# Gates of the last two chunk pairs by seven block products instead of eight

## The chip, the core and the metric

The kernel runs on one core of a Trainium2 chip. The metric is the device time of one execution in microseconds (us), as a median of several runs. The engines of the core are TensorE (PE; PEld is its weight load), VectorE (DVE), ScalarE (ACT), GpSimd (POOL) and SyncE (SP), which here only issues DMAs. Each engine works through its own instructions in order, and an instruction waits for semaphores that others raise.

## What is computed

Linear attention with phi(x) = elu(x) + 1 over 8 batches, 8 heads, 576 positions and head size 64, and behind it a gated feed-forward block on the 4608 tokens of 512 features. Inputs and output are float32.

```python
q_p, k_p = (phi(q), phi(k))
kv = np.einsum('bhsd,bhse->bhde', k_p, v)
z = np.sum(k_p, axis=2)
num = np.einsum('bhsd,bhde->bhse', q_p, kv)
den = np.einsum('bhsd,bhd->bhs', q_p, z)[..., None] + 1e-06
x = (num / den)            # tokens x 512
a = x @ w1                 # 512 -> 1024
b = x @ w2                 # 512 -> 1024
h = a * b @ w3             # 1024 -> 1024
out = h @ w_out            # 1024 -> 512
```

## The kernel before

All matmuls take bfloat16 operands and sum into float32 in PSUM. The product w3 @ w_out is formed once at the start (steps T3 and FW), so each token then needs two gate matmuls (with w1 and w2), an elementwise product and one matmul with the folded 1024 x 512 weights.

The program is a list of steps written out by hand, `ORDER`. A step is a letter code with numbers: `F.5.0` is `s_F(5, 0)`. The last letter names an engine (a ACT, v DVE, p GpSimd; s and b name queues). The steps are issued in the list's order, and each engine keeps that order for its own instructions, so the list sets the order on every engine and in every queue.

- LQ, LK, LV load half a batch of q, k or v (576 KB) through SP's queue into one of 13 `ld` slots, which are handed round in order.
- PT, EX and PM form phi on DVE and ACT; VC casts v.
- KB (line 341, `kv_mm`) forms a batch's kv on TensorE. QD (line 386) transposes phi(q) by a DMA on SP's queue into a `qt` tile.
- NT and ND (line 399, `nd_mm`) form numerators and denominators of three tokens' tiles (128 tokens each) or one; NM (line 405, `over`) divides on DVE. Their PSUM tiles are the two `at` tiles of two banks each; four more `mm` tiles of one bank serve the rest.
- XD (line 463) transposes two tiles of x by a DMA on SP's queue: two XD make a chunk of 512 tokens, x transposed. There are nine chunks, 0 to 8.
- F.c.f (lines 483, 492, 494) makes 128 of the 1024 gate columns of chunk c: four matmuls for side a, four for side b, each 128 x 128 weights against 512 tokens; ACT copies a out of PSUM, and DVE multiplies it with b into `ab`. Chunk 0 is done in halves by FS.
- O.t (lines 536, 543) is one tile's eight matmuls with the folded weights and the copy out; S.t (line 549) stores it by two DMAs of 128 KB. Q.35 is the last tile, in pieces.

In the list F steps of a chunk stand where its two XD are expected to be through, and the loads, phi, KB and NT of later batches are spread between them up to chunk 6.

Of the kernel before, what the change touches and what calls it, by code (L numbers as in the profile page):

```python
# [19 lines left out]
T3.7.0.v LO.0 CO.0.a LO.2 CO.1.v FW.2.0.a T3.7.1.a LO.3 FW.4.0.a CO.3.a LQ.0.0 L3.6 FW.7.0.a  # L23
PT.q.0.0 L3.1 FW.2.1.a FW.4.1.a EX.q.0.0 LQ.0.1 PM.q.0.0 CO.2.p FW.2.2.a FW.7.1.a FW.7.2.v FW.7.3.a
FW.4.2.a FW.4.3.v QP.0.0.v C3.6.a LK.0.0 T3.1.0.a T3.1.1.a PT.q.0.1 FW.2.3.v L3.3 L3.5 T3.6.0.v
T3.6.1.v EX.q.0.1 LK.0.1 FW.1.0.a FW.1.1.a PT.k.0.0 FW.1.2.a PM.q.0.1 FW.6.0.a FW.6.1.v FW.6.2.v
LH.0.0 EX.k.0.0 T3.3.0.a T3.3.1.a FW.1.3.a C3.5.v T3.5.0.a FW.6.3.v EX.k.0.1 PT.k.0.1 LV.0.0 LV.0.1
LH.0.1 FW.3.0.a FW.3.1.v T3.5.1.a FW.3.2.v FW.3.3.v PM.k.0.1 LA.0 LB.6 I.2 CA.0.p CB.6.p LB.7
PM.k.0.0 T3.0.0.a LA.1 FW.5.0.a VC.0.0.a QP.0.1.v FW.0.0.a FW.0.1.a KV.0.0.a LA.2 VC.0.1.v FW.5.1.v
T3.0.1.v KV.0.1.a NT.0 NM.0.0 NM.0.1 CB.7.p FW.0.2.a FW.0.3.a NM.0.2 FW.5.2.a FW.5.3.a LA.3 XP.0.a  # L30
CA.2.p XP.1.v ND.3 LB.2 CA.1.v XP.2.a LB.3 FS.0.0.0.0 FS.0.1.0.0 FS.0.1.1.0 FS.0.0.1.0 LQ.1.1 LK.1.0
XP.3.v FS.0.2.0.0 FS.0.2.1.0 FS.0.2.0.1 FS.0.2.1.1 CB.2.v FS.0.0.0.1 FS.0.0.1.1 FS.0.1.0.1
FS.0.1.1.1 FS.0.3.0.1 CB.3.v PT.q.1.1 CA.3.p F.0.4 EX.q.1.1 PM.q.1.1 PT.k.1.0 LQ.1.0 LV.1.0 PT.q.1.0
EX.k.1.0 FS.0.3.0.0 LK.1.1 F.0.5 F.0.6 PM.k.1.0 VC.1.0.v EX.q.1.0 PM.q.1.0 QP.1.1.a EX.k.1.1
FS.0.3.1.0 PT.k.1.1 LV.1.1 F.0.7 KV.1.0.a LQ.2.1 LQ.3.1 VC.1.1.a QP.1.0.a O.0.a PM.k.1.1 KV.1.1.v
LV.2.0 FS.0.3.1.1 EX.q.3.1 NT.4 NM.4.0 NM.4.1 O.1.a NM.4.2 EX.q.2.1 PT.q.2.1 LK.2.0 XP.4.a ND.7
XP.5.a LK.2.1 EX.k.2.1 LK.3.1 O.2.a PT.q.3.1 PT.k.2.1 LV.3.0 XP.6.v XP.7.v LV.2.1 EX.k.2.0 PM.k.2.1
LV.3.1 O.3.a PT.k.2.0 LQ.2.0 S.0.s LQ.3.0 PM.k.2.0 PM.q.2.1 VC.2.0.v LV.4.1 F.1.0 F.1.1 PT.k.3.1
# [26 lines left out]
def kernel(  # L65
# [36 lines left out]
    def take(kind, key, shape, dtype, name):  # L102
        if kind in free:
            s = slots[key] = free[kind].popleft()
        else:
            s = taken.get(kind, 0) % turns[kind]
            taken[kind] = taken.get(kind, 0) + 1
        pool = ps if kind in ("mm", "at") else sb
        return pool.tile(shape, dtype, tag=f"{kind}{s}", name=name)

    def give(kind, key):
# [415 lines left out]
    def s_FP(c0, f, side, g, e):  # L527
        f_mm(c0, f, side, slice(2 * g, 2 * g + 2))
        if g == 1:
            f_out(c0, f, side)  # L530

    def o_mm(t, cols):
        c0, m = divmod(t, CT)
        o_ps = mm_tile("o_ps")[:, 0:cols.stop - cols.start]
        for f in range(FC):
            nc.tensor.matmul(o_ps, abs_[c0][:, f, m * P:(m + 1) * P], wf_sb[:, f, cols],  # L536
                             start=(f == 0), stop=(f == FC - 1))
# [66 lines left out]
```

## Time and profile before

| | |
|---|---|
| time, median of 3 runs | 240.42 us (240.42 to 240.85) |
| span of the profiled execution | 239.7 us |
| around the span, up to the median | 0.7 us |
| bytes moved by DMA | 55.81 MB |
| read from HBM, written | 38.80 MB, 9.44 MB |

The profile is of one execution. Its views name an engine, a line of the kernel, what is written and what is read (`ab<-a_sb,b_ps`), shapes as partitions x elements, a count, the busy time and the mean time of one in ns, and the idle time before it with what ended that. A chain row has its start, its length, the work and a count. A row of busy times by stretch has for PE, PEld, DVE, ACT, POOL the busy us and the count, then the granted TensorE clock (1.00 is full), the busy share of the 16 DMA engines (which can pass 1 where transfers overlap) and GB/s. A row of waits has who waited for whom: us in total, times, longest. Issue rows of DMAs give KB each and the median us from issue to landing.

### The profile page before, as it was taken

The numbers are of one execution on the slowest core, as the hardware profiler recorded it, in microseconds if no ns is written. First come the engines' busy times: TensorE is split into PE (matmuls) and PEld (weight loads), VectorE is DVE, ScalarE is ACT, GpSimd is POOL, SyncE is SP. The second block draws the span as 40 slices with busy tenths as digits, with TensorE's granted clock in tenths as the row PEclk, the third lists the DMA queues.
The fourth block names the chain that finished last, engine by engine and source line by source line (L and its number), as shares of the span: only waits on it lengthen the run. The fifth ranks groups of instructions, "written<-read, shape, count | busy, mean of one in ns | idle before, by whom it ended". The sixth has DMA issues, their size and how long they took to land.

```text
span 239.7 us, 5540 instructions
## 1 busy us (share of the span) xinstructions
PE 233.2 (97%) x2276; PEld 120.2 (50%) x2276; DVE 151.0 (63%) x278; ACT 115.0 (48%) x173; POOL 8.1 (3%) x15
## 2 busy tenths in 40 slices
PE   8899999999999999999999999999999999999994
PEld 5656668555445444444454444545444444444443
DVE  0347787889999646877862588885546363433341
ACT  2576743979793255568522656424232113321300
POOL 1020053000000000000000000000000000000000
PEclk9999999999999999999999999999999999999999
DMA  6999999999996999999879959965293763005216
GB/s 241 402 406 397 379 375 390 390 390 389 396 332 137 158 357 247 323 406 296 190 106 192 392 123 262 320 116 131 52 178 69 174 157 88 3 0 125 50 24 154
DMA packets 52553, 55.81 MB, mean 233 GB/s; under 512 B 31280, under 2 KB 32560, under 8 KB 52528
## 3 DMA queue, kind: packets, MB, share of 16 engines
q1 hardware_dynamic: 52288, 55.19, 78.5%
q8 instruction: 18, 0.29, 0.5%
q10 hardware_dynamic: 240, 0.26, 0.3%
q14 instruction: 7, 0.06, 0.1%
HBM read 38.80 MB, written 9.44 MB: 201 GB/s over the span
## 4 chain that ended last, share of the span: by engine, by line
PE 96%; DVE 1%; ACT 1%; issue 0%
PE o_ps L536 26%; PE a_ps L483 25%; PE b_ps L483 24%; PE wf_ps L264 6%; PE nd L399 3%; PE w3p L252 3%; PE warm L149 2%; PE kbp L341 2%; PE a_ps L516 2%; PE b_ps L516 2%; PE xp L458 1%; PE qp L369 1%; PE kvp L341 1%; ACT wo_sb L218 0%; ACT w3b L238 0%; DVE w3t L253 0%
## 5 line engine op out<-in xcount | busy, mean ns | idle before, releaser
L483 PEld LDWEIGHTS <-w_sb 128*128 128x128 bf16 x544 | 52.6, 98 | 62.5 <-DVE xt L459 0.3
L494 DVE TENSOR_TENSOR ab<-a_sb,b_ps 128x512 bf16<-128x512 f32 x68 | 46.2, 686 | 39.9 <-PE b_ps L483 38.6
L492 ACT COPY a_sb<-a_ps 128x512 f32<-128x512 f32 x68 | 39.8, 586 | 64.0 <-PE a_ps L483 63.6
L483 PE MATMUL a_ps<-xt,w_sb 128*128 128x512 bf16 x272 | 69.9, 380 | 0.0
L483 PE MATMUL b_ps<-xt,w_sb 128*128 128x512 bf16 x272 | 69.8, 379 | 0.0
L536 PE MATMUL o_ps<-wf_sb,ab 128*128 128x512 bf16 (+2 forms) x304 | 65.2, 368 | 0.0
L536 PEld LDWEIGHTS <-ab 128*128 128x128 bf16 x304 | 28.4, 98 | 31.7 <-issue 0.4
L543 ACT COPY o_sb<-o_ps 128x512 f32<-128x512 f32 x22 | 12.9, 586 | 33.5 <-PE o_ps L536 26.7
L405 DVE TENSOR_TENSOR xn<-nd,r 128x512 bf16<-128x512 f32 (+2 forms) x47 | 23.8, 559 | 0.3
L274 ACT ACTIVATE ek<-k 128x1152 bf16<-128x1152 f32 x16 | 18.7, 1172 | 0.7 <-ACT ek L274 0.7
L274 ACT ACTIVATE eq<-q 128x1152 bf16<-128x1152 f32 x16 | 18.7, 1168 | 0.4 <-DMA q<-in_q_dram 0.4
L543 DVE COPY o_sb<-o_ps 128x512 f32<-128x512 f32 x13 | 9.0, 691 | 15.3 <-PE o_ps L536 12.6
L264 PE MATMUL wf_ps<-wo_sb,w3t 128*128 128x512 bf16 x64 | 15.6, 380 | 0.5 <-ACT wo_sb L218 0.5
L286 DVE TENSOR_SCALAR phq<-q 128x1152 bf16<-128x1152 f32 x16 | 12.0, 755 | 2.7 <-DMA q<-in_q_dram 2.7
L294 DVE TENSOR_TENSOR phk<-phk,ek 128x1152 bf16<-128x1152 bf16 x16 | 11.9, 750 | 1.8 <-ACT ek L274 1.7
L294 DVE TENSOR_TENSOR phq<-phq,eq 128x1152 bf16<-128x1152 bf16 x16 | 12.1, 755 | 1.0 <-ACT eq L274 0.8
L286 DVE TENSOR_SCALAR phk<-k 128x1152 bf16<-128x1152 f32 x16 | 12.0, 753 | 0.0
L264 PEld LDWEIGHTS <-w3t 128*128 128x128 bf16 x64 | 5.9, 98 | 5.8 <-issue 0.7
L328 ACT CAST vt<-v 128x1152 bf16<-128x1152 f32 x7 | 8.1, 1162 | 0.9 <-DMA v<-in_v_dram 0.9
L253 ACT CAST w3t<-w3p 128x512 bf16<-128x512 f32 x7 | 4.0, 587 | 9.3 <-PE w3p L252 7.4
L399 PEld LDWEIGHTS <-qt 64*64 64x64 bf16 x576 | 6.1, 106 | 4.3 <-issue 4.1
L399 PE MATMUL nd<-kv,qt 64*64 64x65 bf16 x576 | 7.6, 194 | 0.4 <-DVE w3t L253 0.4
(57 smaller groups left out, 127.4 us busy)
## 6 DMA issues: line engine op xcount, KB each, us to landing
q<-in_q_dram SPq DMA_DIRECT2D x16, 576.0 KB, 8.3
k<-in_k_dram SPq DMA_DIRECT2D x16, 576.0 KB, 9.5
v<-in_v_dram SPq DMA_DIRECT2D x16, 576.0 KB, 10.5
out_dram<-o_sb SPq DMA_DIRECT2D x69, 128.0 KB, 2.5
w<-in_moe_w_dram SPq DMA_DIRECT2D x7, 512.0 KB, 10.9
wo<-in_moe_w_out_dram SPq DMA_DIRECT2D x4, 512.0 KB, 8.2
wa<-in_moe_w_dram SPq DMA_DIRECT2D x4, 512.0 KB, 10.7
wb<-in_moe_w_dram SPq DMA_DIRECT2D x4, 512.0 KB, 10.4
```

Source lines behind the costliest of these rows:

```text
L264: nc.tensor.matmul(wfs[i], w3ts[i][:, c, :], wo_sb[:, c, :], start=(c == 0), stop=(c == FC - 1))
L274: nc.scalar.activation(out=t, in_=raw[n, b, h], func=AF.Exp)
L286: (nc.gpsimd if e == "p" else nc.vector).tensor_scalar(out=by_set(n, t), in0=by_set("k", raw[n, b, h]), scalar1=0.0, scalar2=1.0, op0=ALU. ...
L294: nc.vector.tensor_tensor(out=t, in0=t, in1=by_set("k", es[n, b, h]), op=ALU.min)
L399: nc.tensor.matmul(dst[g * R:(g + 1) * R], qts[b, a // 2][rows, j, a % 2 * R:(a % 2 + 1) * R], kvs[b][rows, a // 2, a % 2, :], start=True, ...
L405: nc.vector.tensor_tensor(out=xn[:, :, a0:a1], in0=n4[:, :, :, 0:D], in1=r.unsqueeze(3).to_broadcast([P, 2, a1 - a0, D]), op=ALU.mult)
L483: nc.tensor.matmul(ops_[key][:, tiles.start * P:tiles.stop * P], w[:, w_row(kc), f * P:(f + 1) * P], xts[c0][:, tiles, kc, :], start=(kc = ...
L492: nc.scalar.copy(out=a_sbs[c0, f], in_=ops_[key])
L494: nc.vector.tensor_mul(out=abs_[c0][:, f, :], in0=a_sbs[c0, f], in1=ops_[key])
L516: nc.tensor.matmul(p, w[:, w_row(kc), f * P:(f + 1) * P], xts[c0][:, 2 * g:2 * g + 2, kc, :], start=(kc == 0), stop=(kc == KC - 1))
L536: nc.tensor.matmul(o_ps, abs_[c0][:, f, m * P:(m + 1) * P], wf_sb[:, f, cols], start=(f == 0), stop=(f == FC - 1))
L543: copy_of(e)(out=o_sbs[t], in_=o_ps)
```

## The change

Chunks 5 and 6, and 7 and 8, form two pairs. For a pair the gate of 256 columns (f and f + 4) by 1024 tokens over the 512 features is a product of 2 x 2 blocks on each side. The change forms it in Winograd's way of Strassen's method: seven products of blocks and sums of blocks in place of eight. A product (`WP.c.f.side.i`) is two matmuls of 128 x 128 weights against 512 tokens.

- WS forms four sums of weight blocks for each side, in bfloat16, on DVE (for w1 into the tile of w_out, which is no longer needed; for w2 into `ld` slots). WT forms four differences of blocks of x per pair.
- One PSUM bank takes products 1, 6, 7 and 4 of a side on top of one another (y), one takes 5 and 3 (z), one of the `mm` banks takes 2 (x). After 1, 5 and 6 ACT copies the bank out; after 2, 3 and 7 DVE adds such a copy to the bank; after 4 ACT copies (side a) or DVE multiplies (side b). A product into a bank waits for the read of what is there.
- The products of the other three blocks, a times b, have both factors in SBUF: they are on GpSimd (24 of them). The results go into `ld` slots (`abq`), from which O reads.
- RB closes the pool of the two `at` tiles and opens four one-bank tiles (`bk`) in their place, for y and z.

The list of steps is the same up to the load of q that follows step PT.k.2.0, and another one behind it.

```diff
+PAIRS = (5, 7)
+WIDE = ()
...
-    free = {"ld": deque(range(13)), "mm": deque(range(4)), "at": deque(range(2))}
+    at_pool = ctx.enter_context(ExitStack())
+    pools = {"mm": ps, "at": at_pool.enter_context(tc.tile_pool(name="at", bufs=1, space=bass.MemoryType.PSUM))}
...
+    free = {"ld": deque(range(13)), "mm": deque(range(4)), "at": deque(range(2)), "bk": deque(range(4))}
...
-            nc.tensor.matmul(o_ps, abs_[c0][:, f, m * P:(m + 1) * P], wf_sb[:, f, cols],
+            nc.tensor.matmul(o_ps, ab_of(c0, f)[:, m * P:(m + 1) * P], wf_sb[:, f, cols],
...
+    def s_WS(side, i, e):
+        w = (w1_sb, w2_sb)[side]
+        a, b, op = {1: (w_half(w, 0, 1), w_half(w, 1, 1), ALU.add),
+                    2: (ws_of(side, 1), w_half(w, 0, 0), ALU.subtract),
+                    3: (w_half(w, 0, 0), w_half(w, 0, 1), ALU.subtract),
+                    4: (w_half(w, 1, 0), ws_of(side, 2), ALU.subtract)}[i]
+        (nc.gpsimd if e == "p" else nc.vector).tensor_tensor(out=ws_of(side, i), in0=a, in1=b, op=op)
+
+    def s_WT(c0, i, e):
+        b11, b12, b21, b22 = x_half(c0, 0), x_half(c0 + 1, 0), x_half(c0, 1), x_half(c0 + 1, 1)
+        a, b = {1: (b12, b11), 2: (b22, xs_of(c0, 1)), 3: (b22, b12), 4: (b21, xs_of(c0, 2))}[i]
+        (nc.gpsimd if e == "p" else nc.vector).tensor_tensor(out=xs_of(c0, i), in0=a, in1=b, op=ALU.subtract)
+
+    def w_mm(ps, c0, f, side, i, first):
...
+        for r in range(2):
+            nc.tensor.matmul(ps, lhs[:, r, f * P:(f + 1) * P], rhs[:, :, r, :],
+                             start=(first and r == 0), stop=(r == 1), skip_group_check=not first)
...
+    def w_add(c0, f, side, ps, tmp, c, g, e):
+
+        nc.vector.tensor_tensor(out=tmp, in0=ps, in1=tmp, op=ALU.add)
+        if side == 0:
+            wtmp[c0, f, "a", c, g] = tmp
+        else:
+            (nc.gpsimd if e == "p" else nc.vector).tensor_mul(
+                out=w_ab(c0, f, c, g), in0=wtmp.pop((c0, f, "a", c, g)), in1=tmp)
+
+    def s_RB(e):
+
+        at_pool.close()
+        pools["bk"] = at_pool.enter_context(tc.tile_pool(name="bk", bufs=1, space=bass.MemoryType.PSUM))
+
+    def s_WP(c0, f, side, i, e):
+        q = c0, f, side
+        bank = q + ("z" if i in (3, 5) else "x" if i == 2 else "y",)
...
+        w_mm(ps, c0, f, side, i, i in (1, 2, 5))
+        if i in (1, 5, 6):
+            t = wtmp[q + (i,)] = w_tmp({1: "e", 5: "phq", 6: "phk"}[i], "p" + str(i) + "ab"[side])
+            nc.scalar.copy(out=t, in_=ps)
+        elif i == 2:
+            w_add(c0, f, side, ps, wtmp.pop(q + (1,)), 0, 0, e)
+            give("mm", bank)
+        elif i == 3:
+            w_add(c0, f, side, ps, wtmp.pop(q + (6,)), 1, 0, e)
+            give("bk", bank)
+        elif i == 7:
+            w_add(c0, f, side, ps, wtmp.pop(q + (5,)), 1, 1, e)
+        elif side == 0:
+            t = wtmp[c0, f, "a", 0, 1] = w_tmp("a_sb", "p4a")
+            nc.scalar.copy(out=t, in_=ps)
+        else:
+            nc.vector.tensor_mul(out=w_ab(c0, f, 0, 1), in0=wtmp.pop((c0, f, "a", 0, 1)), in1=ps)
```

In the list itself the part around the start of the new stage reads:

```diff
+XD.6.0 NM.30.1 NM.30.2 O.18.a WS.1.4.v NT.33 NM.33.0 WT.5.1.v WT.5.3.v WT.5.2.v NM.33.1 NM.33.2 RB
+WP.5.0.0.1 O.19.a WP.5.0.0.5 WP.5.0.1.5 XD.7.1 WP.5.0.0.2 WP.5.0.1.1 WP.5.0.0.6 WT.5.4.v WP.5.0.0.3
```

and the gates of chunks 1 to 4 stand on TensorE in the order F.1.5 F.1.7 F.1.1 F.1.2 F.1.4 F.1.6 ND.8 KB.2 F.1.0 F.1.3 NT.9 KB.3 O.7 O.6 NT.12 O.5 O.4 F.2.7 NT.15 F.2.5 F.2.6 F.2.2 F.2.4 F.2.3 F.2.1 F.3.4 F.2.0 F.3.7 KB.4 O.8 F.3.5 F.3.0 NT.18 KB.5 F.3.3 O.10 F.3.6 F.3.1 NT.21 O.9 O.11 F.4.6, then F.4.0 F.4.4 F.4.5 KB.6 NT.24 F.4.1 F.3.2 F.4.2 F.4.3 O.13 NT.27 KB.7 F.4.7 NT.30 O.15 O.18 NT.33 and the first product.

On SP's queue, between the third store of the program and the second pair of x transposes, there stood before (q, k, v are loads, o_sb stores, qt the transposes of phi(q), QD, and xt those of x, XD):

```order
L549 DMA out_dram<-o_sb 64x512 x4
L386 DMA_TRANSPOSE qt<-phq 128x9x128 x4
L463 DMA_TRANSPOSE xt<-xn 128x8x128 x2
L158 DMA v<-in_v_dram 128x2x576
L158 DMA q<-in_q_dram 128x2x576
L549 DMA out_dram<-o_sb 64x512 x2
L158 DMA k<-in_k_dram 128x2x576
L158 DMA q<-in_q_dram 128x2x576
L158 DMA k<-in_k_dram 128x2x576
L463 DMA_TRANSPOSE xt<-xn 128x8x128 x2
```

The two pairs of xt here are XD.2 and XD.3, with five loads between them. In the change the same stretch of SP's queue, from the first QD of batch 2 to the first half of XD.3, reads:

```order
L401 DMA_TRANSPOSE qt<-phq 128x9x128 x2
L173 DMA q<-in_q_dram 128x2x576 x2
L401 DMA_TRANSPOSE qt<-phq 128x9x128 x2
L173 DMA q<-in_q_dram 128x2x576
L478 DMA_TRANSPOSE xt<-xn 128x8x128
L576 DMA out_dram<-o_sb 64x512 x2
L478 DMA_TRANSPOSE xt<-xn 128x8x128
L173 DMA v<-in_v_dram 128x2x576
L173 DMA k<-in_k_dram 128x2x576 x4
L173 DMA v<-in_v_dram 128x2x576
L478 DMA_TRANSPOSE xt<-xn 128x8x128
```

Loads of later batches have moved ahead of the transposes: three between the QD and XD.2, six between XD.2 and XD.3, and the transposes stand singly. From the load of q at which the lists part up to XD.4.1, 25 loads stand in the queue in the change; up to XD.4.1 of before 17 do.

On TensorE, at the end of NT.33 (nd is its PSUM tile, qt a weight), there stood before the output matmuls of O.26:

```order
L399 LDWEIGHTS qt
L399 MATMUL nd<-kv,qt 64x65
L536 LDWEIGHTS ab
L536 MATMUL o_ps<-wf_sb,ab 128x512
L536 LDWEIGHTS ab
```

In the change NT.33 is followed by the first product, into bank y of side a (wya), and then by O.19; the semaphores that an instruction waits for stand in brackets:

```order
L414 MATMUL nd<-kv,qt 64x65
L642 LDWEIGHTS w_sb [waits DMAHW7_49,DMAHW2_49,DVE_49]
L642 MATMUL wya<-xt,w_sb 128x512 [waits PE_49]
L642 LDWEIGHTS w_sb
L642 MATMUL wya<-xt,w_sb 128x512
L557 LDWEIGHTS ab
L557 MATMUL o_ps<-wf_sb,ab 128x512 [waits Activation_49]
```

The weight load in front of the first product now waits for DVE; its count is that of the last division of NT.33. What DVE has there is, from NT.33's first instruction on:

```order
L446 TENSOR_SCALAR r<-nd 128x14
L447 TENSOR_SCALAR r<-nd 128x10
L448 RECIPROCAL r<-r 128x24
L420 TENSOR_TENSOR xn<-nd,r 128x512
L631 TENSOR_TENSOR xs<-xt 128x1024 x2
L631 TENSOR_TENSOR xs<-xt,xs 128x1024
L420 TENSOR_TENSOR xn<-nd,r 128x2x192
L420 TENSOR_TENSOR xn<-nd,r 128x2x64
L420 TENSOR_TENSOR xn<-nd,r 128x512
L662 TENSOR_TENSOR p1a<-wxa,p1a 128x512
```

Three WT differences (xs) have come between the divisions (xn) of NT.33; before, the same divisions stood together.

More of the change, by code (lines that the diff above doesn't have):

```diff
@@ L27 @@
[L27 to L38, printed above, removed]
@@ L107, in take @@
             taken[kind] = taken.get(kind, 0) + 1
-        pool = ps if kind in ("mm", "at") else sb
+        pool = pools.get(kind, sb)
         return pool.tile(shape, dtype, tag=f"{kind}{s}", name=name)
@@ L530, in s_FP, with ab_of @@
             f_out(c0, f, side)
+    def ab_of(c0, f):
+        for c in range(2):
+            if c0 - c in PAIRS and c0 - c not in WIDE:
+                return quads[c0 - c, f % 4][:, c, f // 4]
+        return abs_[c0][:, f]
     def o_mm(t, cols):
@@ L544, in s_O @@
         give("mm", "o_ps")
+        c0 = t // CT - (t // CT - 1 in PAIRS)
+        if c0 in PAIRS and c0 not in WIDE:
+            n = uses["o", c0] = uses.get(("o", c0), 0) + 1
+            if n == 2 * CT:
+                for f in range(FC // 2):
+                    give("ld", ("abq", c0, f))
     def store(queues, t, o_sb, cols):
@@ new lines, in w_tmp, with w_ab @@
+    def w_tmp(kind, name):
+        if kind == "a_sb":
+            return take(kind, None, [P, NCH], F32, name)
+        t = take(kind, None, [P, HW], BF16, name)
+        return t.bitcast(F32)[:, 0:NCH]
+    def w_ab(c0, f, c, g):
+        if c0 in WIDE:
+            if c0 + c not in abs_:
+                abs_[c0 + c] = take("ab", None, [P, FC, NCH], BF16, "ab")
+            return abs_[c0 + c][:, f + 4 * g]
+        if (c0, f) not in quads:
+            quads[c0, f] = late(("abq", c0, f), 4).rearrange("p (c g n) -> p c g n", c=2, g=2)
+        return quads[c0, f][:, c, g]
```

115 lines of the change are left out of this document (89 added, 26 removed).

## The prediction

> **What bounds the kernel now.** I read the page first (busy shares, the chain that ended last), then the busy time by stretch, then what TensorE waited for, then the chain in order of time.
>
> ```profile
> span 239.7 us, 5540 instructions
> PE 233.2 (97%) x2276; PEld 120.2 (50%) x2276; DVE 151.0 (63%) x278; ACT 115.0 (48%) x173; POOL 8.1 (3%) x15
> PE 96%; DVE 1%; ACT 1%; issue 0%
> ```
> ```profile
> 60.00:80.00 20.00, 20.00 (x291) 9.88 (x290) 18.94 (x34) 13.45 (x22) 0.00 (x0) 1.00 0.98 270
> 120.00:140.00 20.00, 20.00 (x219) 9.45 (x205) 10.91 (x24) 8.08 (x14) 0.00 (x0) 1.00 0.88 209
> 200.00:220.00 20.00, 20.00 (x95) 9.00 (x93) 7.52 (x11) 5.26 (x9) 0.00 (x0) 1.00 0.12 28
> ```
> ```profile
> PE warm L149 <- DVE zero L136: 1.2, 1, 1.2
> PE wf_ps L264 <- ACT wo_sb L218: 0.5, 1, 0.5
> ```
>
> The reader is to see that TensorE is full: 20.00 of 20 us in each stretch (first column after the length), at granted clock 1.00, and that its longest wait in all, 1.2 us, is the first one. The time is the sum of TensorE's own work, so fewer matmuls shorten it as long as nothing makes TensorE wait. The columns behind are DVE, ACT and GpSimd busy time, then clock, DMA share and GB/s: from 60 to 80 us DVE (18.94 of 20) and the DMA engines (0.98) are nearly full too. That is where the change moves work to.
>
> **What the seven products save.**
>
> ```profile
> 203.30 0.86 PE a_ps L483 x4
> 103.22 1.73 PE o_ps L536 x8
> 119.57 0.78 PE kbp L341 x72
> 190.59 0.51 PE nd L399 x48
> 59.93 0.86 PE a_ps L483 x4
> ```
>
> These rows of the chain (start, length, count) price each TensorE step: four gate matmuls 0.86 us, so 0.216 each; a gate step F (both sides) 1.73; an output step O 1.73; KB 0.78; NT 0.5. A pair of chunks takes 2 x 64 gate matmuls before and 4 blocks x 2 sides x 7 products x 2 = 112 in the change. Two pairs save 32 x 0.216 = **6.9 us**. O, KB, NT and the rest keep their counts.
>
> **What it adds beside TensorE.**
>
> ```profile
> L494 DVE TENSOR_TENSOR ab<-a_sb,b_ps 128x512 bf16<-128x512 f32 x68 | 46.2, 686 | 39.9 <-PE b_ps L483 38.6 <-ACT a_sb L492 0.8 <-issue 0.3
> L294 DVE TENSOR_TENSOR phk<-phk,ek 128x1152 bf16<-128x1152 bf16 x16 | 11.9, 750 | 1.8 <-ACT ek L274 1.7
> L492 ACT COPY a_sb<-a_ps 128x512 f32<-128x512 f32 x68 | 39.8, 586 | 64.0 <-PE a_ps L483 63.6
> L222 POOL CAST w_sb<-wa 128x1024 bf16<-128x1024 f32 x3 | 3.3, 1085 | 18.9 <-DMA wa<-in_moe_w_dram 18.9
> ```
>
> Per block of 28 matmuls (6.05 us of TensorE) ACT makes 7 copies at 586 ns, 4.1 us, and DVE six sums and one product out of PSUM at 686, 4.8 us. Both fit under 6.05. The 24 products of two SBUF tiles on GpSimd are not in the trace: the nearest row is its cast of 1024 columns at 1.09 us, so 0.54 for 512 columns from below and, with two fp32 inputs, 1.09 from above. I take 1.09, the whole row: three a block, 3.3 us, also hidden; they would show only beyond 2.0 each. The 16 block sums (WS, WT, 1024 bf16 columns) are priced by the 1152-column bf16 row: 750 x 1024/1152 = 0.67 us, from above twice the 512-column row, 1.37. I take 0.67, the same kind of operation.
>
> In the Strassen stage a product is two matmuls, 0.43 us, and one bank is written, read, and written again (1, 6, 7, 4). A read-back costs about 0.9 us from matmul to reader's end (0.69 and the handover), and the order keeps two or more other products between a pair that depends so; where DVE is one operation late TensorE loses up to 0.69. Nothing from below, 16 such chains x 0.69 = 11 from above; DVE has 56 x 0.686 + 4 x 0.67 + 8 copies x 0.69 = 46.6 us of work beside 48.4 us of products and 13 O steps, 70.9 in all, so I take **0.8**, near the empty end.
>
> **What it moves: the transfers.** All of NT and KB now stands ahead of the stage, so the loads of K, Q and V, and the DMA transposes behind them, have to be done some 25 us of TensorE work earlier. They share one queue, in which transposes stand behind loads.
>
> ```profile
> 40.00:70.00 30.00, 30.00 (x385) 16.03 (x384) 27.00 (x51) 25.62 (x37) 0.00 (x0) 1.00 1.05 391
> 75.00:77.00 2.00, 2.00 (x80) 1.10 (x81) 2.00 (x4) 0.52 (x1) 0.00 (x0) 1.00 0.00 0
> 92.00:94.00 2.00, 2.00 (x11) 0.89 (x10) 1.03 (x2) 0.82 (x2) 0.00 (x0) 1.00 1.44 89
> ```
> ```profile
> 52.20 1.19 SPq L158 DMA_DIRECT2D q<-in_q_dram  x1
> ```
> ```profile
> v<-in_v_dram SPq DMA_DIRECT2D x2, 576.0 KB, 12.1
> ```
> ```profile
> DMA packets 2593, 0.65 MB, mean 259 GB/s; under 512 B 2593, under 2 KB 2593, under 8 KB 2593
> ```
>
> To be seen: the DMA engines are full to 70 us, at 391 GB/s; a load of 576 KB costs 1.51 us, a tile's two stores (256 KB) 0.67. The last row is the stretch from 72.0 to 74.5 us, in which only transposes ran, at 259 GB/s: 1.14 us for a phi tile (QD, 295 KB), 1.01 for a half x chunk (XD, 262 KB). The load issued at 52.20 is the last before the orders part; its neighbours landed 12.1 us after issue, so it lands at 64.3. From 75 to 77 the queue of before is empty: room that the change fills.
>
> Going from transposes back to loads costs more: from 92 to 94 only 89 GB/s moved. So 0 to 1.5 us a switch; I take 0.6, nearer to nothing, because the change issues most transposes one by one with loads already queued behind them.
>
> Up to XD.2.1, which F.2.7 needs, the change queues 9 loads, 3 store pairs, 4 QD, 2 XD, 2 switches: 13.6 + 2.0 + 4.6 + 2.0 + 1.2 = 23.4, so it lands at 87.7. TensorE would be there at 59.93 (quoted row, F.1) + 8 F + 4 O + ND + 2 KB + 2 NT = 83.5: **4.2 late**. Up to XD.3.0, which F.3.4 needs: 7 loads, 1 pair, 2 XD, 2 switches more, 14.5, so 102.2 against 83.5 + 7 F + NT = 96.1: 6.1 late. Up to XD.4.1, which F.4.6 needs: 9 loads, 5 pairs, 4 QD, 2 XD, 5 switches, 26.6, so 128.8 against 96.1 + 8 F + 4 O + 2 KB + 2 NT = 119.4: **9.4 late** in total (the delays contain each other). Without any price for switches it is 123.4, 4.0 late; at 1.5 each 136.9, 17.5 late. Behind it the queue has under 20 us of work for 24 us of TensorE, so nothing more is late.
>
> **The wait that it adds.** RB closes the pool of the two-bank tiles; the first product's weight load then waits for DVE's last read of them, NM.33.2, and all of TensorE's queue stands behind it, O.19 first, which needs nothing of it.
>
> ```profile
> 191.24 0.16 DVE L431 TENSOR_SCALAR r<-nd 128x14 f32<-128x14 f32 x1
> 191.32 0.16 DVE L432 TENSOR_SCALAR r<-nd 128x10 f32<-128x10 f32 x1
> 191.51 0.30 DVE L433 RECIPROCAL r<-r 128x24 f32<-128x24 f32 x1
> 191.85 1.95 DVE L405 TENSOR_TENSOR xn<-nd,r 128x512 bf16<-128x512 f32 x4
> ```
>
> Before, NT.33 ends at 191.1 on TensorE and DVE is through with it at 193.8, 2.7 us later; O.26 hides that. In the change three WT sums (2.0) stand between its parts and nothing hides it: **4.7 us**. From below 2.7 + 3 x 0.6 = 4.5; with sums at 1.37 it is 6.8.
>
> **Sum.** The profiled execution's span is 239.7; 0.7 lies around it up to the median of 240.4, and I let that stay. 240.4 - 6.9 + 9.4 + 4.7 + 0.8 = **248.4 us**.
>
> **Rivals.**
> - *The transfers keep up.* If transposes don't wait for the loads ahead, or the queue packs better than 391 GB/s, so that XD.4.1 lands by 119.4, only the wait at RB is left: 240.4 - 6.9 + 4.7 + 0.8 = 239.0, faster. For it: in the trace no x chunk comes late. Against: the order of before has that empty queue at 75, and 17 loads ahead of XD.4 where the change has 25; it decides where 25 loads, 9 pairs, 8 QD and 6 XD take under 55.1 us (64.3 to 119.4), and without a switch they cost 59.0. Chance 0.15.
> - *Everything is covered,* RB too, since DVE reads NM.33 before TensorE is there: 240.4 - 6.9 = 233.5 to 236. Against: NM.33 needs NT.33, the instruction just ahead. Chance 0.04.
> - *Switches at full price, and a stage held by DVE.* 17.5 late, 6.8 at RB, 3 in the stage: 240.4 - 6.9 + 27.3 = 260.8; with one of them, 254 to 257. For it: from F.1 to NM.33 DVE has 32 gate products x 0.69, 52 operations of 1152 columns x 0.75, 9 NT x 2.6 and 11 block sums x 0.67, 92 us less some overlap of neighbours, in 84 us of TensorE, so a late load is hard to make up. Chance 0.13.
> - *The gates are not fewer in time* (a product's two matmuls at other than 0.43): their shapes are those of L483, so I give it no chance of its own.
>
> One rule speaks against GpSimd's part. In the trace GpSimd is idle (0.00) in all stretches after 40 us, so no row shows it beside DVE. The Trainium skill, SBUF — State Buffer, section "Who interferes with whom", says that a Vector instruction with two SBUF inputs and a GpSimd instruction that reads SBUF exclude each other for the whole instruction. Here that would touch the four WT sums inside the stage alone (the other DVE sums have one input in PSUM): at most 4 x 1.09 = 4.4 us of DVE, in a stage where it has 24 to spare, and if all of it reached TensorE 252.8. It lies inside the range, at a chance of 0.03.
>
> **How the numbers follow.** Forecast 0.65 (242.5 to 254), with 0.15, 0.04, 0.13 and 0.03 as above. The range of 8 in 10 leaves out the fast end below 239 and the far end above 256: **239 to 256**. A measurement tells about 0.2% from no change. Faster 0.17 (the two fast rivals, less a little of the first), same 0.03, slower 0.80.
>
> **What would show it.** Saving: 512 gate matmuls of 128x512 in place of 544, still 216 ns apart. Transfers: TensorE's waits name DMA xt, ahead of F.2.7, F.3.4 and F.4.6, some 9 us together, and the DMA share stays near 1 from 72 to 125 us. RB: one wait of about 4.7 us on DVE xn ahead of the first product. Stage: ACT and DVE under 75% busy, few waits on p tiles. I am wrong if TensorE has no wait on xt (then 239), or if the waits within the stage pass 5 us together.

## The result and the profile after

| | before | after |
|---|---|---|
| time, median (four runs each, on one chip) | 240.57 us (240.42 to 240.85) | 258.38 us (257.44 to 260.57) |
| ratio | | 1.0739, 95% interval 1.068 to 1.0799 |
| span of the profiled execution | 239.7 us | 256.7 us (its own time 258.76) |

The change makes the kernel 7.4% slower. The sign was forecast, the size was not: 258.4 against 248.4, and outside the range of 239 to 256. Ratios leave out runs in a slower state that some executions show, which matters for the sixth experiment alone: two of its four runs, the profiled one among them, were in it.

First the page of the changed kernel: span, TensorE's busy share, the granted clock in 40 slices (tenths), and who stands on the chain that ended last.

```profile
span 256.7 us, 5592 instructions
PE 230.5 (90%) x2244; PEld 117.5 (46%) x2244; DVE 177.0 (69%) x318; ACT 127.4 (50%) x197; POOL 38.9 (15%) x39
PEclk9999999999999999997999999799999999999998
PE 70%; DMA 14%; DVE 10%; issue 2%; ACT 1%; SPq 1%; DVEq 0%; ACTq 0%
```

TensorE is busy for 2.7 us less than before, but over a span 17.0 longer. It is no longer alone on the chain, where transfers now hold 14% and DVE 10%, and in two slices its clock falls.

Then what TensorE waited for from F.1 to RB (first fence) and behind that (second): who for whom, us in total, times, longest.

```profile
PE nd L414 <- DMA qt<-phq: 4.1, 3, 2.0
PE a_ps L498 <- DMA xt<-xn: 3.6, 2, 1.9
PE kbp L356 <- DVE ab L509: 2.1, 2, 1.8
PE b_ps L498 <- DVE ab L509: 1.9, 2, 1.6
```
```profile
PE wya L642 <- DVE xn L420: 4.6, 1, 4.6
PE wya L642 <- DVE xs L631: 0.9, 1, 0.9
PE wya L642 <- DVE p5a L662: 0.6, 1, 0.6
```

Last, five stretches of the changed kernel (from the first matmul of F.1 to that of F.4.6, on to the end of NT.33, the wait at RB, the stage up to the last matmul, and the end), and the end of the kernel before.

```profile
59.13:133.70 74.57, 62.84 (x794) 29.65 (x793) 62.07 (x115) 43.13 (x61) 0.00 (x0) 0.98 1.12 303
133.70:158.77 25.07, 24.76 (x432) 12.33 (x432) 19.54 (x42) 10.53 (x17) 0.00 (x0) 1.00 0.76 144
158.77:163.35 4.58, 0.00 (x2) 0.00 (x1) 4.29 (x10) 0.11 (x1) 0.00 (x0) 0.94 0.89 191
163.35:251.75 88.40, 86.94 (x408) 39.46 (x408) 51.12 (x76) 34.96 (x63) 30.91 (x24) 0.98 0.28 63
251.75:256.70 4.95, 0.00 (x0) 0.00 (x0) 0.29 (x1) 0.00 (x0) 0.00 (x0) 0.82 0.61 161
```
```profile
236.16:239.70 3.54, 0.00 (x0) 0.00 (x0) 0.29 (x1) 0.00 (x0) 0.00 (x0) 0.93 0.54 151
```

The account goes by these stretches, counted in TensorE's steps at 1.726 us for an F or an O. The work up to F.4.6 is 59.5 us at the prediction's prices and some 60.3 with what NT and KB really take: before, the stretch from F.1 (59.77) to the last matmul (236.16) holds 176.4 us, of which 64 F, 31 O and Q are 165.7, so nine NT, ND and six KB are 10.7, about 1 more than at 0.5 and 0.78. So 74.57 holds **14.3** of lateness. The next stretch has 24.7 of work and loses 0.4, RB costs **4.6**, the stage has 48.4 + 20 O + Q = 84.7 of work and loses **3.7**, and the end is **1.4** longer. With the start of F.1 0.6 earlier and 6.9 saved: 14.3 + 0.4 + 4.6 + 3.7 + 1.4 - 0.6 - 6.9 = 16.9, of the 17.0 between the spans.

### The profile page after: what moved, and what is told of

The parts are those of the page before. It is cut to its first block, busy times and chain, and to the rows that moved or that the text cites. A ratio compares the mean times of both kernels' runs of the same rounds, so it can differ in the third digit from the quotient of the medians.

```text
span 256.7 us, 5592 instructions
## 1 busy us (share of the span) xinstructions
PE 230.5 (90%) x2244; PEld 117.5 (46%) x2244; DVE 177.0 (69%) x318; ACT 127.4 (50%) x197; POOL 38.9 (15%) x39
## 4 chain that ended last, share of the span: by engine, by line
PE 70%; DMA 14%; DVE 10%; issue 2%; ACT 1%; SPq 1%; DVEq 0%; ACTq 0%
PE o_ps L557 20%; DMA qt<-phq 8%; PE a_ps L498 8%; PE b_ps L498 7%; DMA xt<-xn 6%; PE wf_ps L279 6%; PE wyb L642 5%; PE wya L642 5%; PE wzb L642 3%; PE wza L642 3%; PE w3p L267 2%; PE warm L164 2%; PE nd L414 2%; DVE ab L509 2%; PE a_ps L531 1%
## 5 line engine op out<-in xcount | busy, mean ns | idle before, releaser
L498 PEld LDWEIGHTS <-w_sb 128*128 128x128 bf16 x288 | 27.7, 99 | 39.8 <-DMA xt<-xn 4.6
L498 PE MATMUL a_ps<-xt,w_sb 128*128 128x512 bf16 x144 | 37.9, 386 | 3.6 <-DMA xt<-xn 3.6
L498 PE MATMUL b_ps<-xt,w_sb 128*128 128x512 bf16 x144 | 37.2, 381 | 1.9 <-DVE ab L509 1.9
L557 PE MATMUL o_ps<-wf_sb,ab 128*128 128x512 bf16 x160 | 38.2, 387 | 0.0
L507 ACT COPY a_sb<-a_ps 128x512 f32<-128x512 f32 x36 | 20.9, 586 | 21.5 <-PE a_ps L498 21.3
L509 DVE TENSOR_TENSOR ab<-a_sb,b_ps 128x512 bf16<-128x512 f32 x36 | 24.3, 683 | 9.3 <-PE b_ps L498 6.9
L557 PE MATMUL o_ps<-wf_sb,abq 128*128 128x512 bf16 (+2 forms) x144 | 29.1, 355 | 0.0
L557 PEld LDWEIGHTS <-ab 128*128 128x128 bf16 x160 | 15.3, 100 | 18.1 <-issue 1.9
L557 PEld LDWEIGHTS <-abq 128*128 128x128 bf16 x144 | 13.5, 98 | 14.5
L642 PEld LDWEIGHTS <-w_sb 128*128 128x128 bf16 x96 | 9.3, 98 | 16.7 <-DVE xn L420 4.7
L666 POOL TENSOR_TENSOR abq<-p6a,p6b 128x512 bf16<-128x512 f32 x8 | 10.6, 1329 | 13.7 <-DVE p6b L662 7.1
## 6 DMA issues: line engine op xcount, KB each, us to landing
wb<-in_moe_w_dram SPq DMA_DIRECT2D x4, 512.0 KB, 10.7
```

What stands on the lines that cost most here:

```text
L498: nc.tensor.matmul(ops_[key][:, tiles.start * P:tiles.stop * P], w[:, w_row(kc), f * P:(f + 1) * P], xts[c0][:, tiles, kc, :], start=(kc = ...
L507: nc.scalar.copy(out=a_sbs[c0, f], in_=ops_[key])
L509: nc.vector.tensor_mul(out=abs_[c0][:, f, :], in0=a_sbs[c0, f], in1=ops_[key])
L557: nc.tensor.matmul(o_ps, ab_of(c0, f)[:, m * P:(m + 1) * P], wf_sb[:, f, cols], start=(f == 0), stop=(f == FC - 1))
L642: nc.tensor.matmul(ps, lhs[:, r, f * P:(f + 1) * P], rhs[:, :, r, :], start=(first and r == 0), stop=(r == 1), skip_group_check=not first)
L666: (nc.gpsimd if e == "p" else nc.vector).tensor_mul(out=w_ab(c0, f, c, g), in0=wtmp.pop((c0, f, "a", c, g)), in1=tmp)
```

## The experiments

Each was timed beside the kernel before on the same chip (241.0 to 241.6 us there) and has four to six runs, the third one run. Differences to the change are of medians from two chips; the runs of one kernel lie more than 3 us apart in places (255.44 to 258.55 in the first), so a difference under some 2 us between two experiments is not secure. Spans are those of the profiled executions. Step names are those of the list.

**1. The moves alone.**

```diff
-PAIRS = (5, 7)
+PAIRS = ()
 ... NT.33 NM.33.0
-WT.5.1.v WT.5.3.v WT.5.2.v NM.33.1 NM.33.2 RB WP.5.0.0.1 O.19.a WP.5.0.0.5 ...
+NM.33.1 NM.33.2 O.19.a XD.7.1 O.12.a ... F.5.0 XD.8.1 F.5.1 ... F.8.7 ... Q.35
```

> The new list up to NT.33 word for word (the sums WS too), and behind it the gates of chunks 5 to 8 as plain steps F, eight block products in place of seven, with no RB, no sums WT and no product on GpSimd. Theory that the moves cost the time (transfers late): the first matmul of F.4.6 stays at about 133.7 us and the end of NT.33 at about 158.7, the waits on DMA qt and xt stay at some 7 to 8 us together, and the time is that of the changed kernel (258.4) plus 6.9 for the saved matmuls, less 4.6 for the wait at RB and 3 to 5 for the stage and its end: 255 to 258. Rival, that the stage with seven products costs it: the moves are worth little and the time is 241 to 247.

Measured: 257.06 us, ratio 1.0654 (1.0585 to 1.0723). F.4.6 and NT.33 stand where they stood, and the waits on qt and xt are 3.9 and 2.6 us, a little less than expected. The rows of the timeline are F.4.6's first matmuls, with the idle time ahead of them and what ended it in brackets, and NT.33:

```profile
133.79 1.04 PE L486 MATMUL a_ps<-xt,w_sb 128*128 128x512 bf16 x4 [1.61 <-DMA xt<-xn]
158.23 0.58 PE L402 MATMUL nd<-kv,qt 64*64 64x65 bf16 x48
```

So the moves alone cost 15.9 us, and the rival (the stage costs it) falls. The change is slower still, by 1.3 us in the medians and 2.8 in the spans (253.9 and 256.7): its saving of 6.9 is used up by RB, the stage and the end, 4.6 + 3.7 + 1.4 = 9.7.

**2. The wait at RB covered.**

```diff
-WT.5.1.v WT.5.3.v WT.5.2.v NM.33.1 NM.33.2 RB WP.5.0.0.1 O.19.a ... O.12.a
+NM.33.1 NM.33.2 WT.5.1.v WT.5.3.v WT.5.2.v O.19.a O.12.a RB WP.5.0.0.1 ...
```

> The changed kernel with NM.33.1 and NM.33.2 ahead of the three sums WT on DVE and with O.19 and O.12 ahead of the first product on TensorE. Theory that the wait at RB lies bare and draws a slow stretch of TensorE behind it: the wait of 4.6 us on DVE xn goes, and with it the 1.6 us by which the first product and O.19 ran long, so the time falls by 4.6 to 6.2, to 252.2 to 253.8. Rival, that DVE is behind there in any case: the wait moves to product 5 on the sum xs and the time falls by less than 2 us. A third reading, that the slow stretch has nothing to do with the wait: 4.6 less, and the low granted clock near 163 us stays.

Measured: 253.56 us, ratio 1.0507 (1.0471 to 1.0543), 4.8 less than the change, and 5.6 by the spans (251.1 and 256.7). The wait is gone, and only 0.3 us on another tile (p6a) takes its place. The same 3.5 us of the clock show what happened behind the wait: in the change (first fence), here (second), and in the third experiment, which keeps the wait, behind its own first product at 153.56 (third). The column ahead of the DMA share is the granted clock.

```profile
163.35:166.85 3.50, 3.50 (x10) 1.31 (x11) 0.00 (x0) 0.59 (x1) 0.00 (x0) 0.59 0.71 147
```
```profile
163.35:166.85 3.50, 3.20 (x16) 1.36 (x14) 2.52 (x4) 2.28 (x6) 0.00 (x0) 1.00 0.92 207
```
```profile
153.56:157.06 3.50, 3.28 (x9) 1.30 (x11) 0.00 (x0) 0.59 (x1) 0.00 (x0) 0.56 0.67 148
```

With the wait TensorE starts again at 0.56 to 0.59 of its clock, without it at 1.00, so the third reading falls: the bare wait of 4.6 us costs about 1.4 more, since 3.5 us at 0.59 do the work of 2.1.

**3. Half of the late loads left out.**

```diff
 ...
     def load(key, src, cols):
+        if key[0] in ("q", "k", "v") and key[1] > 3:
+            n = whole.setdefault(key[:2], key)
+            if n != key:
+                raw[key] = raw[n]
+                return
 ...
```

This kernel leaves out input data, so its output is not the one asked for; only its time is of use.

> The changed kernel with half of the loads of q, k and v for batches 4 to 7 left out (12 of 24, 7 MB): the second half of the heads is taken from the same tile as the first, and every other instruction stays. Theory that the volume in the queue of transfers makes TensorE late: 12 loads at 1.5 us leave the queue, some 10 of them ahead of XD.4.1, so F.4.6 starts 10 to 14 us earlier, at 120 to 124, its wait on xt is gone, and the time falls to 244 to 249. Rival, that DVE or the issue of transposes on SP holds the row of steps, not the volume: F.4.6 stays beyond 130 and the time over 254.

Measured: 249.72 us in its single run, 8.7 less than the change, just outside what was expected (249) and far from the rival. No step waits for xt; F.4.6 starts at 123.69, 10.0 earlier, and the first product 9.8 earlier:

```profile
123.69 1.04 PE L510 MATMUL a_ps<-xt,w_sb 128*128 128x512 bf16 x4
153.56 0.69 PE L654 MATMUL wya<-xt,w_sb 128*128 128x512 bf16 x2 [4.58 <-DVE xn L432]
```

KB.5's wait on DVE falls with it, from 1.8 to 0.3. What DVE stood for there in the change was a transfer too, a phq tile that a late QD still read (the last row's bracket):

```profile
118.43 1.21 PE L356 MATMUL kbp<-vt,phk 64*64 64x65 bf16 x71 [1.79 <-DVE ab L509]
```
```profile
116.15 0.76 DVE L301 TENSOR_SCALAR phq<-q 128x1152 bf16<-128x1152 f32 x1 [3.12 <-DMA qt<-phq]
```

TensorE's other wait on DVE, 1.6 us at 65.17, is still there at 1.3. So the late loads carry most of the lateness, some 10 us of it, also where the wait names DVE. Whether by their volume or by standing ahead of the transposes this run does not tell: both go with them.

**4. GpSimd's products on DVE.**

```diff
-WP.5.0.1.2.p WP.5.0.1.3.p ...
+WP.5.0.1.2.v WP.5.0.1.3.v ...
```

> The changed kernel with the 24 products of two SBUF tiles on DVE in place of GpSimd. Theory that GpSimd's products and DVE's sums of two SBUF tiles shut each other out: the three sums WT of 1.39, 1.75 and 1.43 us inside the stage fall to about 0.68, the wait of 0.9 us on xs goes, and as DVE has 51 us of work in 88 us of the stage its further 24 x 0.7 = 17 us stay hidden: time 256.5 to 258.4. Rival, that these sums are long for another reason (a late x chunk, the clock): they stay over 1.3 us without GpSimd. Second rival, that GpSimd relieves DVE: more waits of TensorE on DVE p5, p6 and p1 tiles, and 259 to 263.

Measured: 265.0 us, ratio 1.095 (1.0885 to 1.1016), 6.6 slower than the change: slower than either reading gave. Both mechanisms are there. First three sums WT in the change, of which the first had no GpSimd product beside it; then two groups of products and sums in the change (count, shortest, median, longest in ns); then all eight sums without GpSimd.

```profile
169.09 0.68 DVE L631 TENSOR_TENSOR xs<-xt,xs 128x1024 bf16<-128x1024 bf16 x1
195.56 1.75 DVE L631 TENSOR_TENSOR xs<-xt,xs 128x1024 bf16<-128x1024 bf16 x1
200.22 1.43 DVE L631 TENSOR_TENSOR xs<-xt,xs 128x1024 bf16<-128x1024 bf16 x1
```
```profile
L666 POOL TENSOR_TENSOR abq<-p6a,p6b x8: 1265/1272/1732, 174.8 to 238.4; 128x512 bf16<-128x512 f32 x8
L662 DVE TENSOR_TENSOR p5a<-wya,p5a x8: 676/690/692, 171.9 to 235.3; 128x512 f32<-128x512 f32 x8
```
```profile
L630 DVE TENSOR_TENSOR xs<-xt x4: 680/686/686, 161.7 to 199.6; 128x1024 bf16<-128x1024 bf16 x4
L630 DVE TENSOR_TENSOR xs<-xt,xs x4: 681/684/687, 162.9 to 205.3; 128x1024 bf16<-128x1024 bf16 x4
```

A sum of two SBUF tiles that meets a product of GpSimd takes up to 1.75 in place of 0.68, and GpSimd's product up to 1.73 in place of 1.27; a sum with one input in PSUM (L662) stays at 0.69. This is the rule of the Trainium skill, SBUF — State Buffer, section "Who interferes with whom", and the trace agrees: a Vector instruction with two SBUF inputs and a GpSimd instruction that reads SBUF keep each other out. In the change TensorE's two waits on DVE in the stage, 0.9 on xs and 0.6 on p5a, stand right behind the sums of 1.75 and 1.43; how much of them is the lock is not shown, as waits of that size are there without GpSimd too. But GpSimd takes more off DVE than that: without it TensorE waits 1.5 for p6b, 1.4 for p5a, 0.9 for abq and 0.6 for xs. From the first product to the end this kernel takes 98.4 us against 93.3, so 5.0 of the 6.6 belong to GpSimd; 1.6 were lost ahead, between F.4.6 and NT.33, where the clock fell in this execution.

**5. The last pair alone, on the list of before.**

```diff
-PAIRS = (5, 7)
+PAIRS = (7,)
 (list of before up to NT.27, with WS beside F.4.0 to F.4.3, F.5.6 and F.5.7; then)
+NM.27.0 S.18.s XD.6.1 NM.27.1 EX.q.7.0 O.19.a PM.q.7.0 EX.q.7.1 NM.27.2 O.20.a PM.q.7.1 QD.7.0 QD.7.1 XD.7.0 O.21.v WS.1.3.v O.22.a
+F.6.0 WS.1.4.v F.6.1 S.19.s S.20.s F.6.2 NT.30 NM.30.0 NM.30.1 NM.30.2 XD.7.1 F.6.3 S.21.s F.6.4 S.22.s NT.33 NM.33.0 NM.33.1 XD.8.0 NM.33.2 XD.8.1
+F.6.5 F.6.6 F.6.7 O.23.a S.23.s RB (products 1, 2, 5, 6, 3, 7 of both sides, the 4 behind the next block's 1 and 2) ...
```

> The list of the kernel before with the last pair alone (chunks 7 and 8) by seven products: no load is moved; phi(q) of batch 7 and its QD come some 5 us earlier, NT.30 and NT.33 stand ahead of F.6.3 and F.6.5, and three F steps and O.23 cover the division, the x transposes and the sums WT before the first product. Theory that seven products pay where nothing has to be moved past the loads: 16 gate matmuls less at 0.216 are 3.45 us, no wait at RB, 0.5 to 2 us lost in the stage: 1.5 to 3 us faster than the kernel before, ratio 0.987 to 0.994. Rival, that the stage costs by itself what it saves (read-backs of the one bank, the end of the program): ratio 0.998 to 1.008, with more than 3 us of waits on p tiles.

Measured: **238.04 us** against 241.06, ratio 0.9885 (0.986 to 0.9909): 3.0 us (1.2%) faster than the kernel before, clear of the noise, and the fastest here. TensorE is full again, and from 160 us to the end it has one wait:

```profile
span 236.0 us, 5581 instructions
PE 229.2 (97%) x2260; PEld 118.1 (50%) x2260; DVE 161.1 (68%) x297; ACT 123.1 (52%) x190; POOL 23.8 (10%) x27
PEclk9999999999999999999999999999999999999998
```
```profile
PE wza L636 <- ACT p4a L690: 0.3, 1, 0.3
```

16 gate matmuls less are 3.45, and 3.0 of it arrives. The stage itself does not eat its saving.

**6. The late loads on a queue of their own.**

```diff
-        nc.sync.dma_start(out=dst, in_=src)
+        (nc.gpsimd if key[0] in ("q", "k", "v") and key[1] > 3 else nc.sync).dma_start(out=dst, in_=src)
```

> The changed kernel with the loads of batches 4 to 7 issued on GpSimd's queue, so that transposes and stores stand alone on SP's. Theory that the order in one queue makes the x transposes late: they land about 3 us after issue, TensorE's waits on DMA xt and qt (7.7 us) and the one of KB.5 go, F.4.6 starts at 119 to 123, time 246 to 251. Rival, that the DMA engines are full whatever the order: the transposes share them with the loads, phi comes late on DVE instead, NT.33 still ends at 155 to 160, time 255 to 260.

Measured: 294.15 us (289.57 to 295.72), ratio 1.2095 (1.202 to 1.2169). Both readings miss. The transposes of phi(q) do not come sooner beside the loads but far later: first TensorE's wait and the group's median from issue to landing here, then the same group in the change.

```profile
PE nd L414 <- DMA qt<-phq: 33.0, 3, 16.7
qt<-phq SPq DMA_TRANSPOSE x12, 12.0
```
```profile
qt<-phq SPq DMA_TRANSPOSE x12, 6.4
```

The Trainium skill, DMA: Bandwidth & Descriptors, section "Queues, rings and completion order", says that each DMA engine takes turns between its queues, a packet from each. By that rule a transpose, which the prediction's DMA row shows as packets under 512 B, gives way to a load's packet after each of its own; the rows agree with it, and no run here counts the turns. Nor does a run separate them from other costs of the second queue, such as the 0.72 us that GpSimd takes to issue a load. One queue in order is the better arrangement here.

**7. The last stores at their tiles** (with RB covered as in 2).

```diff
-O.31.v O.33.v S.31.s O.30.a O.29.v S.29.s O.28.v S.30.s O.32.v S.33.s O.34.a S.28.s S.32.s S.34.b Q.35
+O.31.v S.31.s O.33.v S.33.s O.30.a S.30.s O.29.v S.29.s O.28.v S.28.s O.32.v S.32.s O.34.a S.34.b Q.35
```

> The kernel of the second experiment (wait at RB covered) with each of the last seven stores right behind its tile. Theory that the end grew because stores stand late in SP's queue and the last copy of ACT waits for a slot of o_sb: the stretch from the last matmul to the end of the span falls from 5.0 to about 3.5 us, as before, and the time by 1.4 to about 252.2. Rival, that the last tile's own store sets the end: no change, 253.6.

Measured: 252.92 us, ratio 1.0502 (1.046 to 1.0545). The stretch behind the last matmul does what was expected, 4.97 in the second experiment (first row) and 3.41 here:

```profile
246.13:251.10 4.97, 0.00 (x1) 0.00 (x0) 0.29 (x1) 0.00 (x0) 0.00 (x0) 0.70 0.61 160
```
```profile
247.89:251.30 3.41, 0.00 (x0) 0.00 (x0) 0.29 (x1) 0.00 (x0) 0.00 (x0) 0.99 0.54 154
```

The medians differ by 0.6 only and the intervals overlap, so a gain in time is not shown. In the profiled execution F.4.6 starts where it did in the second experiment (134.01 and 134.02), but the clock falls behind its longer wait on xt (3.0 in place of 2.1) and the first product comes 1.75 later.

**8. Both pairs, with the order of before** (behind RB the products in rounds, as in 5).

```diff
-(list of the change up to RB)
+(list of before up to NT.33, without F.5 and F.6, the 45 steps F and O left spread evenly over the places of its 70)
```

> Both pairs by seven products, as in the change, but with loads, phi, QD, XD, KB and NT in the order of the kernel before, where each load stands shortly ahead of its use; the 32 gates of chunks 1 to 4 and O.4 to O.16 are spread evenly between them up to NT.33, O.17 and O.18 cover RB, and the products stand in rounds of 1, 2, 5, 6, 3, 7, with the 4 of a block behind the next block's 1 and 2. Theory that the volume in the queue bounds the start of the stage (some 83 us of transfers behind 66 us on the clock, whatever their order): NT.33 ends at 147 to 152, against 143 where TensorE never waits and 158.7 in the change, the stage and its end lose under 1 us, time 237 to 242. Rival, that the order written in the change is what costs: NT.33 ends at 145 or earlier and the time is 234.5 to 236.5. Third, that any list of this kind is as late as that of the change: NT.33 beyond 155, time over 244.

Measured: 276.45 us, ratio 1.1464 (1.139 to 1.1537): the third reading, and worse. NT.33 starts at 180.73. In the page's row of GB/s in 40 slices (6.85 us each) the queue is nearly empty in the 19th, with 8:

```profile
GB/s 279 409 404 384 375 388 389 390 333 398 278 89 105 371 238 365 370 107 8 199 386 197 360 187 154 89 77 153 45 0 0 0 2 77 24 55 77 96 151 137
```

This list lets the queue run dry, so it is no test of volume against order. It shows only that this one list is worse than that of the change.

**9. Two x transposes ahead of loads not yet due** (on the kernel of 7).

```diff
-F.2.7 NT.15 LK.5.1 NM.15.0 LK.6.1 LK.6.0 LV.4.0 ... XD.3.0
+F.2.7 NT.15 XD.3.0 LK.5.1 NM.15.0 LK.6.1 LK.6.0 LV.4.0 ...
-XD.4.0 NT.21 LQ.6.1 LK.7.0 ... XD.4.1
+XD.4.0 XD.4.1 NT.21 LQ.6.1 LK.7.0 ...
```

> The kernel of the seventh experiment (RB covered, stores at their tiles; 252.9 us) with two x transposes ahead of loads that are not due yet on SP's queue: XD.4.1 ahead of LQ.6.1 and LK.7.0, XD.3.0 ahead of LK.5.1, LK.6.1, LK.6.0 and LV.4.0. Theory that the order of loads and transposes makes TensorE late: the two waits on DMA xt (3.6 to 4.9 us) go, NT.33 ends that much earlier, time 248.5 to 249.8. Rival, that the queue is full in any case: what passes behind is later by as much, and the time comes back as waits on qt or on DVE: 252 to 253.5.

Measured: 252.36 us, ratio 1.0442 (1.0396 to 1.0488), 0.6 under the seventh with overlapping intervals. Three of its six runs took 250.93 to 251.28 us; the profiled one is not of these (253.44). In it the waits on xt are gone, as meant, and others have come in their place (the longest from F.1 to the stage):

```profile
PE nd L413 <- DMA qt<-phq: 4.6, 3, 2.1
PE a_ps L497 <- ACT o_sb L563: 3.0, 1, 3.0
PE b_ps L497 <- DVE ab L508: 2.6, 2, 2.0
PE kbp L355 <- DVE ab L508: 2.0, 2, 1.8
```

What was passed in the queue comes later by as much: F.4.6 starts at 137.42, against 134.01 in the seventh, as ACT's copy ahead of it stood 5.2 us for a store. In this execution that is the rival. All six runs miss what the theory gave (248.5 to 249.8); a gain of up to some 2 us in the others stays possible.

**10. A fifth phq tile** (on the kernel of 7): `"phq": 4` becomes `"phq": 5`.

> The kernel of the seventh experiment with five phq tiles in place of four. Theory that a late transpose reaches TensorE by way of DVE too: in the change DVE stands 3.1 us before a phq tile that a QD still reads, and KB.5 waits 1.8 us for DVE's gate product behind it; with a fifth tile DVE's wait there is under 1 us, KB.5's under 0.5, and NT.33 ends 1 to 2 us earlier, time 251 to 252. Rival, that the same lateness comes back at the next transpose: DVE's wait goes, TensorE's waits on xt grow by as much, and the time stays at 252.5 to 253.5.

Measured: 253.61 us, ratio 1.051 (1.0464 to 1.0555): no gain. DVE's wait for a QD is gone and KB.5's with it, and xt grows, from 4.9 to 5.5:

```profile
PE a_ps L497 <- DMA xt<-xn: 5.5, 2, 4.5
PE kbp L355 <- DVE ab L508: 0.3, 1, 0.3
```

The rival again: freeing one place where the late queue shows moves the wait to the next one. F.4.6 starts 1.2 us earlier (132.80), but ahead of it TensorE now waits 4.5 us in one piece, and behind it the clock is 0.50 for 3.5 us.

## Why the prediction was right in sign and short in size

- **What seven products save (6.9): right.** 3.0 of 3.45 arrive in the fifth experiment, where nothing else changes much. Two products in the timeline of the change (start, length, count) stand 0.43 us apart, as priced:

```profile
178.14 0.59 PE L642 MATMUL wyb<-xs,ws 128*128 128x512 bf16 x2
178.57 0.59 PE L642 MATMUL wxa<-xt,w_sb 128*128 128x512 bf16 x2
```

- **The transfers (9.4): the mechanism right, the size not. This term failed.** Its theory, that one loaded queue makes TensorE late ahead of the stage, is borne out by the first and third experiments. Its size is 14.3. F.3.4 and F.4.6 both start on a wait for xt, so their starts show when XD.3.0 and XD.4.1 were through (in the change):

```profile
103.95 1.04 PE L498 MATMUL a_ps<-xt,w_sb 128*128 128x512 bf16 x4 [1.77 <-DMA xt<-xn]
133.70 1.04 PE L498 MATMUL a_ps<-xt,w_sb 128*128 128x512 bf16 x4 [1.87 <-DMA xt<-xn]
```

  The sum of the queue had put them at 102.2 and 128.8, so the 4.9 that are missing are the queue's own: 1.8 up to F.3.4, and the rest behind it, in a stretch priced at 26.6 us that took 29.8. The step with the least ground is the 0.6 for a switch from transposes to loads, out of a range up to 1.5: the five switches in this stretch would have to cost 1.2 each to make it up. But the sum also took the queue as never empty, and it was not. Behind the QD at 112.32, whose issue alone took SP 2.81 us, the DMA engines are at 0.39 and move 106 GB/s:

```profile
114.00:116.00 2.00, 1.48 (x15) 0.54 (x12) 0.00 (x0) 1.54 (x3) 0.00 (x0) 1.00 0.39 106
```

  No run here separates the price of a switch from such gaps, so how the 4.9 divide stays open. The names of the waits were forecast wrongly too: 11.7 us of waits are 4.1 on qt, 3.6 on xt and 4.0 on DVE, where the prediction expected some 9 on xt alone, from F.2.7 on (F.2.7 did not wait). Behind them TensorE ran slow, 3.5 us at a clock of 0.52, which is 1.7 us of work:

```profile
118.50:122.00 3.50, 3.50 (x78) 1.91 (x78) 3.43 (x9) 0.95 (x3) 0.00 (x0) 0.52 1.11 237
```

  Together they are 13.4 of the 14.3, but they are no further terms beside the queue: what TensorE loses earlier it mostly waits less for xt at F.4.6. In the seventh experiment the clock stays at 1.00 in that place, and F.4.6 comes no earlier, behind a longer wait:

```profile
134.01 1.04 PE L497 MATMUL a_ps<-xt,w_sb 128*128 128x512 bf16 x4 [3.03 <-DMA xt<-xn]
```

  That nothing more is late behind F.4.6 held: that stretch loses 0.4.
- **The wait at RB (4.7): right,** 4.58 in the trace. The slow clock behind it, about 1.4, was counted nowhere. Without both the time falls by 4.8 (5.6 by the spans) in the second experiment.
- **The stage (0.8): too small, 3.7.** About 1.4 of it is that slow clock, 1.5 are the waits for xs and p5a. The rest, under 1, was not followed up. What it said of the engines there holds: DVE is busy 51.12 of 88.40 us, ACT 34.96. GpSimd's product, taken at 1.09 from a bound that was to hold from above, takes 1.27; that is still under the 2.0 from which it would show.
- **The end: not in the sum.** Stores of earlier tiles stand late in SP's queue, and ACT's last copy stood 7.4 us for one of them. That is 1.4 us, shown by the trace of the seventh experiment.
- **What lies around the span** was put at 0.7. In all runs of the kernel before that carry their span it is 1.74 to 1.94; by that the span of 239.7 belongs to an execution of some 241.5, about 1 us above the median. The sum starts from the median, so this does not touch it.
- **The rivals.** That the transfers keep up is refuted by the waits. The lock of SBUF, at a chance of 0.03 and 4.4 us, exists and costs TensorE at most the 1.5 of its waits for xs and p5a; there are five WT sums inside the stage, not four, and four of them met a product of GpSimd. The far rival (260.8) was nearest in time, by its late queue and not by DVE holding the stage. One outcome does not show that a chance of 0.13 was too small, but the choice behind it was thinly grounded: the lateness was bounded by 4.0 and 17.5 and taken at 9.4 without a run that prices a switch, and an empty stretch of the queue could only add to it.

What stays open beside the price of a switch: how much of the 14.3 a better list could win back. The ninth and tenth experiments changed single places only, and the eighth let the queue run dry.

## What to carry to other kernels

A saving on the bound engine is worth what is left when the work that hid its transfers has been taken away: here 27.6 us of gate steps (F.5 and F.6) went behind NT.33, and with them the cover of a queue that was already full to 70 us. The fifth experiment suggests to apply such a change where no load has to be due earlier (the last pair alone keeps 3.0 of its 3.45 us). Check each pool that is closed for what must be read before it. When a queue is late, its waits carry several names and stand in for one another: go by when the last transfer lands, and price each kind of turn in the queue, and its gaps, from a row before trusting the sum.

## What the runs showed of the hardware

- **The clock falls behind short idle time.** Behind 4.6 us of idle time TensorE starts at 0.56 to 0.59 of its clock for 3.5 us. Behind single waits on xt the same came after 4.48 us in the tenth experiment, 3.03 in the seventh and 2.53 in the fourth (3.5 us at 0.50, 0.53 and 0.60, in the last two from about 1 us after work had begun again). It also fell to 0.52 from 118.5 behind a stretch in which it was busy for 1.62 of 4.03 us, with no single wait over 1.8:

```profile
114.40:118.43 4.03, 1.62 (x55) 0.77 (x53) 2.17 (x4) 2.70 (x3) 0.00 (x0) 1.00 0.88 258
```

  In the seventh experiment the waits there are nearly the same (2.2 us in place of 2.4) and the clock stays at 1.00, and so it does behind the wait of 2.97 in the ninth, so it does not follow each time. The Trainium skill, TensorE: Matmul & The Clock Gate, Part 1, gives half clock behind an idle window of about 3.4 us; the wait at RB agrees, the stretch at 118.5 shows that it can also come with less.
- **SP itself is held by transposes.** Issuing a QD took SP 1.36 us in the median before and 2.79 in the change (shortest, median and longest in ns; before first), so that all behind it on SP was issued later too:

```profile
L386 SPq DMA_TRANSPOSE qt<-phq x12: 1242/1362/2040, 68.5 to 175.8; - x12
```
```profile
L401 SPq DMA_TRANSPOSE qt<-phq x12: 1273/2790/4283, 66.6 to 145.3; - x12
```

- **A second queue was no way past a full one here.** With the loads on GpSimd's queue the transposes' median landing went from 6.4 to 12.0 us, and TensorE waited 33 us for them.
